# An adaLN block with linear attention on one core: the second modulation vector copied by columns, the first k products of four token tiles run block by block, and the second chunk's transposes put one token tile later

## The chip, the cores and the metric

The kernel runs on one core of a Trainium2 chip. The metric is the device time of one execution in microseconds (us): the median of three runs is 570.62 us (570.37 to 571.47). Beside these runs one execution was recorded by the hardware profiler; it took 570.02 us, and the profile's times are counted from the start of its span.

The engines are TensorE (PE in the rows; PEld are its weight loads), VectorE (DVE), ScalarE (ACT), GpSimd (POOL) and SyncE (SP), which here issues the transfers. Each works through a queue of its own.

## What is computed

The inputs are x (2048 tokens by 512), a condition vector c of 512, and weights. Six modulation vectors of 512 come from `silu(c) @ w_mod`: sa, ca, ga for the attention half, sb, cb, gb for the feed-forward half.

```python
mod = (_silu(c) @ w_mod).reshape(c.shape[0], 6, 1, -1)
h = _layernorm(x, axis=-1) * (1 + ca) + sa
x = x + ga * _A_ref(h, A_wqkv, A_wo)      # linear attention, 32 heads of 16, phi(k), phi(q)
h = _layernorm(x, axis=-1) * (1 + cb) + sb
x = x + gb * _B_ref(h, ...)               # (h W_gate * h W_up) W_down, width 1376
```

In the attention q, k, v are products of h with three 512 x 512 weights. phi(t) is t + 1 for positive t and exp(t) otherwise, plus 1e-6. Over all tokens `kv` sums the products of phi(k) and v, and `z` sums phi(k); a token's output is phi(q) times kv, divided by phi(q) times z, and goes through wo. The change lies in the start of the attention half: ca and sa, the first normalised h, and the first rows of k.

## The kernel before

**Tiling.** The 2048 tokens are four chunks of 512, each of four token tiles of 128 (sixteen tiles, numbered i = 0 to 15). The 512 model columns are four blocks of 128 (b = 0 to 3). A PSUM bank holds 128 x 512 values; there are eight, four in the pool `ps_acc` and four in the pool `ps_w` (`acc_bank()` and `bank()`).

**Split products.** Every float32 operand of a large product is split into a rounded high half and a low half (what is left over): ScalarE copies the high half (`split`, L183), VectorE subtracts to get the low half (L184). One product of a 128-row block is then three TensorE instructions: high by high, high by low, low by high.

**The start.** Chunk 0 is normalised (`Norm`: statistics on VectorE L225 and L226, the power -1/2 on GpSimd L234, the factor `nmr` on VectorE L237, and the scaled tile, called xhat, on ScalarE L243) and turned by TensorE so that the columns lie on the partitions (L257). Meanwhile VectorE multiplies c into the weights of the vectors ca and sa (L159, L161); four small TensorE products (L166, two rows each in the profile) turn the sum into four columns of a PSUM bank, one for each block, and one VectorE instruction (`col_out`, L171) copies them out. Then for each block `modulated` (L259) lets ScalarE write f = scale * xhat + shift (L262), makes its high half h (a VectorE cast, L270, or a second ScalarE instruction, L272) and its low half on VectorE (L273). Fillers (`keep_on`, L143) are products whose result nobody reads, put on TensorE between the small products.

**First products of k.** L365 to L389 write the order out by hand: the copy of sa, the halves of the weight blocks of k (`split_raw(raw_k[b])`) and `modulated` of the four blocks by turns, then `product2` (L200), which runs tiles 0 and 1 together, block after block. Between them stand the statistics of chunk 1 and, for tile 0, the split of xhat (`k_split_x`), `k_phi` (two ScalarE instructions, Relu L291 and Exp L292, then VectorE L295) and the split of phi(k) (`k_split`: kh on ScalarE, L318, kl on VectorE, L319). ScalarE's xhats 0 and 1 of chunk 1 come last.

**The loop over tiles** (L421 to L469). For tile i it issues the product of k for tile i + 2 (`proj`, L196 to L198), for some tiles a product of q, the splits for tile i + 1, the phi of tile i + 2, and `t_tile(i)`: twelve products (L327 to L329) that add xhat by phi(k) into four banks called T. In the first two tiles of a chunk (j = 0 and 1) half of `t_tile` is followed by the transposes of two column blocks of the next chunk (L250) and their `modulated`, then by the other half. At the end of a tile weights are split or modulation vectors summed (`extra`).

**What sets the order.** The schedule is manual: each engine's instructions stand in the order of the source. The waits between engines come from the tiles that they read and write, and a PSUM bank or an SBUF buffer is taken again when its last reader is done. Behind the loop lie the attention's output and the feed-forward half; no line of them is changed.

Of the kernel before, what the change touches and what calls it, by code (L numbers as in the profile page):

```python
# [8 lines left out]
F32 = mybir.dt.float32  # L9
F32R = mybir.dt.float32r  # L10
AF = mybir.ActivationFunctionType
ALU = mybir.AluOpType
AX = mybir.AxisListType

P = 128
# [7 lines left out]
def tile_adaln_block(  # L23
# [12 lines left out]
    nc = tc.nc  # L36
# [3 lines left out]
    KD = D // P  # L40
    NJ = 4
    CH = NJ * P
    NCH = S // CH
# [35 lines left out]
    def acc_bank():  # L79
        return T(ps_acc, "acc")  # L80

    def bank():
        return T(ps_w, "bank")
# [57 lines left out]
    def keep_on(n):  # L141
        for _ in range(n):
            nc.tensor.matmul(ps_idle, idle[:, :P], idle, start=True, stop=True)  # L143
# [19 lines left out]
    def mod_col(acc, ps):  # L163

        for b in range(KD):
            nc.tensor.matmul(ps[:, b:b + 1], acc[:, b * P:(b + 1) * P], ones[:, 0:1], start=True, stop=True)  # L166
        return ps

    def col_out(v, ps, add):
        t = consts.tile([P, KD], F32, name=f"col{v}")  # L170
        nc.vector.tensor_scalar(t, ps[:, :KD], add, None, op0=ALU.add)  # L171
        return t
# [13 lines left out]
    def split_raw(raw, shape=(P, D), low=None):  # L186
        h = B("w", shape, F32R)
        l = B("w", shape, F32R)
        split(raw, h[:raw.shape[0]], l[:raw.shape[0]], low)
        return h, l  # L190
# [6 lines left out]
            nc.tensor.matmul(ps, ah, bl, start=False, stop=False)  # L197
            nc.tensor.matmul(ps, al, bh, start=False, stop=i == n - 1)  # L198

    def product2(pss, pairs):  # L200

        n = len(pairs[0])
        for i in range(n):
            for ps, p in zip(pss, pairs):
                (ah, al), (bh, bl) = p[i]
                nc.tensor.matmul(ps, ah, bh, start=i == 0, stop=False)
                nc.tensor.matmul(ps, ah, bl, start=False, stop=False)
                nc.tensor.matmul(ps, al, bh, start=False, stop=i == n - 1)

    def cut(pair, a, b):  # L210
        return pair[0][:, a:b], pair[1][:, a:b]

# [84 lines left out]
    def k_split_x(i):  # L297
        ch, j = divmod(i, NJ)
        kx[i] = [B("xh", dt=F32R), B("xl", dt=F32R)]
        split(norm[ch].n[j], *kx[i])  # L300

    def k_phi(i, ps):
        phi = B("phi")
        phi_a(ps, phi)
        phi_b(ps, phi)
        phk[i] = phi
# [56 lines left out]
    mod_acc(acc_sa, raw_sa, [0, 1, 2, 3])  # L363
    ca = col_out(1, ps_ca, 1.0)
    keep_on(4)  # L365
    ps_sa = mod_col(acc_sa, acc_bank())
    keep_on(9)
    wk.append(split_raw(raw_k[0]))
    sa = col_out(0, ps_sa, 0.0)
    nx = Norm(xts[1])  # L370
    nx.stats(0)
    n0.modulated(ca, sa, 0, cast=nc.vector)
    wk.append(split_raw(raw_k[1]))
    n0.modulated(ca, sa, 1, cast=nc.vector)
    wk.append(split_raw(raw_k[2]))
    n0.modulated(ca, sa, 2)
    nx.stats(1)
    wk.append(split_raw(raw_k[3]))
    n0.modulated(ca, sa, 3)
    ps0, ps1 = acc_bank(), acc_bank()  # L380
    product2((ps0, ps1), [[(cut(n0.t[k], j * P, (j + 1) * P), wk[k]) for k in range(KD)] for j in range(2)])
    nx.stats(2, 3)
    nx.rstd_of()
    k_split_x(0)
    k_phi(0, ps0)
    nx.nmr_of()
    k_phi(1, ps1)
    k_split(0)
    nx.xhat(0, 1)  # L389

    tacc = [acc_bank() for _ in range(KD)]
    rows, cols = {}, {}
# [24 lines left out]
             13: lambda: (mod_part(5, 0, 1, 2), cols.update({4: col_out(4, mod_col(accs[4], bank()), 1.0)})),  # L417
             14: lambda: (mod_part(5, 3), wo_s.extend(split_raw(x) for x in raw_o)), 15: lambda: rows.update({5: mod_row(5, accs[5])})}
    q_at = {3: 0, 4: 1, 6: 2, 7: 3}
    ahead = {2: proj(2, wk)}  # L420
    for i in range(NT):  # L421
        ch, j = divmod(i, NJ)
        more = ch + 1 < NCH
        if i == 0:
            ahead[3] = proj(3, wk)
        elif i > 1:
            ahead[i + 2] = proj(i + 2, wk) if i + 2 < NT else proj(i + 6 - NT, wq)
        if i in q_at:
            qps = proj(q_at[i], wq)
        if more and j == 0:  # L430
            nx.xhat(2)
        if i + 1 < NT:
            k_split_x(i + 1)
        if more and j == 0:
            nx.xhat(3)
        if i + 1 < NT:
            k_split(i + 1)
        if more and j < 2:
            t_tile(i, 0, 1)
            nx.transpose(2 * j, 2 * j + 1)  # L440
            nx.modulated(ca, sa, 2 * j, 2 * j + 1, cast=nc.vector)
            norm[ch + 1:] = [nx]
        if ch + 2 < NCH and j == 2:
            nx2 = Norm(xts[ch + 2])
            nx2.stats(0, 1)
        if ch + 2 < NCH and j == 3:
            nx = nx2
            nx.stats(2, 3)
            nx.rstd_of()
            nx.nmr_of()  # L450
            nx.xhat(0, 1)
        if i + 2 < NT:
            k_phi(i + 2, ahead.pop(i + 2))
        else:
            q_a(i + 6 - NT, ahead.pop(i + 2))
            q_b(i + 6 - NT)
        if i in q_at:
            q_a(q_at[i], qps)
            q_b(q_at[i])
        if i + 1 < NT:  # L460
            z_add(i + 1)
        if i == NT - 1:
            zps = bank()
            nc.tensor.matmul(zps, ones, zacc, start=True, stop=True)
            zb = consts.tile([P, D], F32, name="zb")
            nc.scalar.activation(zb, zps, AF.Identity, bias=eps_z)
        t_tile(i, *range(2 if more and j < 2 else 0, KD))
        if i in extra:
            extra[i]()  # L469
    ga, gb, sb, cb = rows[2], rows[5], cols[3], cols[4]  # L470
# [727 lines left out]
```

## Time and profile before

| | before |
| --- | --- |
| median of three runs | 570.62 us |
| profiled execution, time | 570.02 us |
| its span | 568.3 us |
| TensorE busy | 560.3 us (99%) |
| VectorE busy | 373.1 us (66%) |
| ScalarE busy | 279.8 us (49%) |
| GpSimd busy | 186.2 us (33%) |

A row of the timeline has the start in us from the span's beginning, the length in us, the engine, the line, the operation with what it writes and reads, and the count; a bracket at its end gives idle time just before it and who ended that. Matmuls are pipelined, so a row's length is longer than the distance to the next one, and their ends are modelled: a wait of TensorE shows best in the distance between starts. Two rows of the same engine may overlap by their start-up.

### The profile page before, as it was taken

How to read it: one execution, taken by the hardware profiler on the slowest of the kernel's cores; microseconds unless marked ns; L12 is line 12 of the kernel's file. 1: busy time of each engine (PE TensorE's matmuls, PEld its weight loads, DVE VectorE, ACT ScalarE, POOL GpSimd, SP SyncE). 2: the span in 40 equal slices, each digit the busy share in tenths (PEclk: the TensorE clock that was granted, in tenths of full speed). 3: DMA queues.
4: the chain of work that ended last, by engine and by line, in shares of the span. 5: the costliest groups of instructions: out<-in, count | busy, mean ns of one | idle time of the engine just before them, and what ended most of it. 6: DMA issues, size and time to landing. Idle time of an engine off the chain costs nothing.

```text
span 568.3 us, 7356 instructions
## 1 busy us (share of the span) xinstructions
PE 560.3 (99%) x2575; PEld 458.8 (81%) x2575; DVE 373.1 (66%) x614; ACT 279.8 (49%) x500; POOL 186.2 (33%) x191
## 2 busy tenths in 40 slices
PE   8999999999999999999989999999999999999997
PEld 6778888888888878878878888787888888888886
DVE  7876868868768876759767777745554434344445
ACT  3785857546456546445865545534333333334110
POOL 2000000000011300000579666665667446556200
PEclk9999999999999999999999999999999999999999
DMA  8900223302301000804208553599336012200004
GB/s 289 374 3 2 74 75 110 114 0 62 93 0 47 29 1 37 260 0 149 57 2 277 180 190 104 202 348 330 115 111 178 26 57 55 57 19 2 0 1 148
DMA packets 50309, 59.34 MB, mean 104 GB/s; under 512 B 6432, under 2 KB 27168, under 8 KB 50272
## 3 DMA queue, kind: packets, MB, share of 16 engines
q1 hardware_dynamic: 50272, 58.87, 32.1%
q8 instruction: 20, 0.33, 0.2%
q14 instruction: 17, 0.14, 0.1%
HBM read 43.12 MB, written 15.73 MB: 104 GB/s over the span
## 4 chain that ended last, share of the span: by engine, by line
PE 89%; DMA 3%; issue 2%; POOL 1%; DVE 1%; ACT 1%; SPq 1%; POOLq 0%; ACTq 0%
PE bank L838 28%; PE acc L914 6%; PE acc L915 6%; PE acc L916 6%; PE acc L614 6%; PE bank L198 5%; PE bank L196 5%; PE bank L197 5%; PE acc L329 3%; PE acc L327 3%; PE acc L328 3%; PE bank L693 2%; PE bank L691 2%; PE bank L692 2%; PE bank L250 2%
## 5 line engine op out<-in xcount | busy, mean ns | idle before, releaser
L838 PE MATMUL bank<-h,w 128*128 128x512 f32 (+1 forms) x798 | 185.5, 390 | 1.8 <-ACT bank L843 1.2
L838 PEld LDWEIGHTS bank<-h,w 128*128 128x128 f32 (+1 forms) x798 | 148.2, 186 | 35.3 <-ACT bank L843 1.7
L843 ACT ACTIVATE bank<-bank 128x512 f32<-128x512 f32 (+1 forms) x38 | 22.1, 583 | 144.8 <-PE bank L838 144.8
L678 DVE TENSOR_TENSOR x<-acc,x 128x512 f32<-128x512 f32 (+1 forms) x73 | 49.1, 684 | 49.0 <-PE acc L916 48.2
L824 POOL TENSOR_TENSOR w<-raw,w 128x256 fp32r<-128x256 f32 (+3 forms) x38 | 42.4, 1117 | 106.4 <-ACT w L817 86.4
L184 POOL TENSOR_TENSOR w<-raw,w 128x512 fp32r<-128x512 f32 (+1 forms) x25 | 34.9, 1399 | 116.0 <-DVE mv L226 87.6
L914 PE MATMUL acc<-w,kh 128*128 128x512 f32 (+2 forms) x154 | 59.6, 387 | 0.0
L915 PE MATMUL acc<-w,kh 128*128 128x512 f32 (+2 forms) x154 | 59.6, 387 | 0.0
L916 PE MATMUL acc<-w,kl 128*128 128x512 f32 (+2 forms) x154 | 59.5, 386 | 0.0
L234 POOL TENSOR_TENSOR rstd<-ve,half 128x4 f32<-128x4 f32 (+1 forms) x9 | 9.4, 1044 | 126.0 <-DVE ve L233 124.5
L184 DVE TENSOR_TENSOR kl<-u,kh 128x512 fp32r<-128x512 f32 (+1 forms) x38 | 26.8, 746 | 33.1 <-ACT kh L183 31.2
L824 POOL TENSOR_TENSOR w<-t,w 128x512 fp32r<-128x512 f32 (+1 forms) x38 | 48.4, 1293 | 0.0
L196 PE MATMUL bank<-w,h 128*128 128x512 f32 x112 | 45.0, 402 | 0.0
L198 PE MATMUL bank<-w,h 128*128 128x512 f32 x112 | 43.9, 392 | 0.0
L197 PE MATMUL bank<-w,h 128*128 128x512 f32 x112 | 43.6, 389 | 0.0
L614 PE MATMUL acc<-w,xh 128*128 128x512 f32 x120 | 38.1, 399 | 0.0
L914 PEld LDWEIGHTS acc<-w,kh 128*128 128x128 f32 (+1 forms) x154 | 28.9, 188 | 6.0
L916 PEld LDWEIGHTS acc<-w,kl 128*128 128x128 f32 (+1 forms) x154 | 28.9, 188 | 5.9
L915 PEld LDWEIGHTS acc<-w,kh 128*128 128x128 f32 (+1 forms) x154 | 28.9, 188 | 5.9
L893 DVE TENSOR_TENSOR u<-bank,u 128x512 f32<-128x512 f32 (+1 forms) x19 | 13.1, 690 | 30.0 <-PE bank L838 30.0
L243 ACT ACTIVATE n<-x,nmr,rstd 128x512 f32<-128x512 f32 x32 | 24.1, 804 | 17.2 <-DVE nmr L237 15.9
L262 ACT ACTIVATE f<-bank,col,col 128x512 f32<-128x512 f32 x28 | 20.7, 775 | 14.5 <-PE bank L250 12.4
(177 smaller groups left out, 1105.1 us busy)
## 6 DMA issues: line engine op xcount, KB each, us to landing
raw<-in_w_mod_dram SPq DMA_DIRECT2D x24, 256.0 KB, 3.7
raw<-in_B_w_down_dram SPq DMA_DIRECT2D x20, 256.0 KB, 2.9
raw<-in_B_w_gate_dram SPq DMA_DIRECT2D x36, 128.0 KB, 3.7
raw<-in_B_w_up_dram SPq DMA_DIRECT2D x36, 128.0 KB, 3.6
x<-in_A_x_dram SPq DMA_DIRECT2D x16, 256.0 KB, 5.4
kept<-f SPq DMA_DIRECT2D x16, 256.0 KB, 2.0
f<-kept SPq DMA_DIRECT2D x16, 256.0 KB, 4.8
side_s<-h SPq DMA_DIRECT2D x16, 256.0 KB, 2.6
```

What stands on the lines that cost most here:

```text
L184: (low or nc.vector).tensor_tensor(l, src, f32(h), op=ALU.subtract)
L196: nc.tensor.matmul(ps, ah, bh, start=i == 0, stop=False)
L197: nc.tensor.matmul(ps, ah, bl, start=False, stop=False)
L198: nc.tensor.matmul(ps, al, bh, start=False, stop=i == n - 1)
L243: nc.scalar.activation(self.n[j], self.tiles[j], AF.Identity, scale=self.rstd[:, j:j + 1], bias=self.nmr[:, j:j + 1])
L614: nc.tensor.matmul(yps[i], x, y, start=False, stop=k == KD - 1 and x is al, skip_group_check=True)
L678: nc.vector.tensor_tensor(xt[:, a:b], dn[j][:, a:b], xt[:, a:b], op=ALU.add)
L824: sub = lambda out, x, y: (on or nc.gpsimd).tensor_tensor(out, x, f32(y), op=ALU.subtract)
L838: mm = lambda x, y, **kw: nc.tensor.matmul(ps, x[:, k], y, skip_group_check=True, **kw)
L914: nc.tensor.matmul(ps, hh[:, a:b], dh[:n, c:d], start=i == 0, stop=False)
L915: nc.tensor.matmul(ps, hh[:, a:b], dl[:n, c:d], start=False, stop=False)
L916: nc.tensor.matmul(ps, hl[:, a:b], dh[:n, c:d], start=False, stop=i == len(hs) - 1)
```

## The change

Three things are edited, all between the sum of sa and the loop's third tile. No transfer and no weight is touched.

1. The four columns of sa are still made by four small products one after the other, but each is copied by an instruction of its own (`sa_out`). The first is copied, block 0 of the weights split and block 0 modulated; then the other three columns are copied. Three fillers follow the small products instead of nine, and all four blocks use VectorE's cast.
2. Tiles 0 to 3 have a bank each from the start (`k_ps`). For blocks 0 and 1 the products of all four tiles run block by block; then blocks 2 and 3 for one tile after the other. `product2` goes, and with it the two `proj` calls for tiles 2 and 3. The statistics of chunk 1, `k_phi` and `k_split` of tiles 0 and 1 are put between in a new order, `k_split(0)` ahead of `k_phi(1)`.
3. The transposes of chunk 1 move from tiles 0 and 1 to tiles 1 and 2. Tile 0 has its twelve T products in one piece; in tile 2 the transposes come first, then all of `t_tile(2)`, then the product of tile 4. The later chunks keep their places.

```diff
-    ps_sa = mod_col(acc_sa, acc_bank())
-    keep_on(9)
-    wk.append(split_raw(raw_k[0]))
-    sa = col_out(0, ps_sa, 0.0)
+    ps_sa = acc_bank()
+    sa = consts.tile([P, KD], F32, name="col0")
+
+    def sa_block(b):
+        nc.tensor.matmul(ps_sa[:, b:b + 1], acc_sa[:, b * P:(b + 1) * P], ones[:, 0:1], start=True, stop=True)
+
+    def sa_out(b):
+        nc.vector.tensor_scalar(sa[:, b:b + 1], ps_sa[:, b:b + 1], 0.0, None, op0=ALU.add)
+
+    def block_in(b):
+        n0.modulated(ca, sa, b, cast=nc.vector)
+
+    def w_in(b):
+        wk.append(split_raw(raw_k[b]))
+
+    for b in range(KD):
+        sa_block(b)
+    keep_on(3)
+    k_ps = [acc_bank(), acc_bank(), bank(), bank()]
+
+    def k_block(b, *js):
+        for j in js:
+            (hh, hl), (wh, wl) = cut(n0.t[b], j * P, (j + 1) * P), wk[b]
+            nc.tensor.matmul(k_ps[j], hh, wh, start=b == 0, stop=False)
+            nc.tensor.matmul(k_ps[j], hh, wl, start=False, stop=False)
+            nc.tensor.matmul(k_ps[j], hl, wh, start=False, stop=b == KD - 1)
+
+    sa_out(0)
+    w_in(0)
+    block_in(0)
+    for b in range(1, KD):
+        sa_out(b)
+    w_in(1)
+    block_in(1)
+    k_block(0, 0, 1, 2, 3)
     nx = Norm(xts[1])
+    w_in(2)
+    block_in(2)
     nx.stats(0)
-    n0.modulated(ca, sa, 0, cast=nc.vector)
-    wk.append(split_raw(raw_k[1]))
-    n0.modulated(ca, sa, 1, cast=nc.vector)
-    wk.append(split_raw(raw_k[2]))
-    n0.modulated(ca, sa, 2)
+    k_block(1, 0, 1, 2, 3)
+    w_in(3)
+    block_in(3)
     nx.stats(1)
-    wk.append(split_raw(raw_k[3]))
-    n0.modulated(ca, sa, 3)
-    ps0, ps1 = acc_bank(), acc_bank()
-    product2((ps0, ps1), [[(cut(n0.t[k], j * P, (j + 1) * P), wk[k]) for k in range(KD)] for j in range(2)])
-    nx.stats(2, 3)
+    k_split_x(0)
+    k_block(2, 0)
+    k_block(3, 0)
+    nx.stats(2)
+    k_phi(0, k_ps[0])
+    k_block(2, 1)
+    k_block(3, 1)
+    nx.stats(3)
     nx.rstd_of()
-    k_split_x(0)
-    k_phi(0, ps0)
+    k_split(0)
+    k_phi(1, k_ps[1])
     nx.nmr_of()
-    k_phi(1, ps1)
-    k_split(0)
     nx.xhat(0, 1)
+    k_block(2, 2)
+    k_block(3, 2)
+    k_block(2, 3)
+    k_block(3, 3)
...
-    ahead = {2: proj(2, wk)}
+    ahead = {2: k_ps[2], 3: k_ps[3]}
+    turn_at = {4 * ch + j: (ch + 1, 2 * j, 2 * j + 1) for ch in range(1, NCH - 1) for j in range(2)}
+    turn_at.update({1: (1, 0, 1), 2: (1, 2, 3)})
     for i in range(NT):
...
-        if i == 0:
-            ahead[3] = proj(3, wk)
-        elif i > 1:
+        done = 0
+        if i > 2:
             ahead[i + 2] = proj(i + 2, wk) if i + 2 < NT else proj(i + 6 - NT, wq)
...
-        if more and j < 2:
-            t_tile(i, 0, 1)
-            nx.transpose(2 * j, 2 * j + 1)
-            nx.modulated(ca, sa, 2 * j, 2 * j + 1, cast=nc.vector)
-            norm[ch + 1:] = [nx]
+        if i in turn_at:
+            to, *ks = turn_at[i]
+            if i != 2:
+                t_tile(i, 0, 1)
+                done = 2
+            nx.transpose(*ks)
+            nx.modulated(ca, sa, *ks, cast=nc.vector)
+            norm[to:] = [nx]
+        if i == 2:
+            t_tile(i, *range(KD))
+            done = KD
+            ahead[i + 2] = proj(i + 2, wk)
...
-        t_tile(i, *range(2 if more and j < 2 else 0, KD))
+        t_tile(i, *range(done, KD))
```

More of the change, by code (lines that the diff above doesn't have):

```diff
@@ L198, in product @@
             nc.tensor.matmul(ps, al, bh, start=False, stop=i == n - 1)
[L200 to L208, printed above, removed]
     def cut(pair, a, b):
@@ L419, in tile_adaln_block @@
     q_at = {3: 0, 4: 1, 6: 2, 7: 3}
-    ahead = {2: proj(2, wk)}
+    ahead = {2: k_ps[2], 3: k_ps[3]}
+    turn_at = {4 * ch + j: (ch + 1, 2 * j, 2 * j + 1) for ch in range(1, NCH - 1) for j in range(2)}
+    turn_at.update({1: (1, 0, 1), 2: (1, 2, 3)})
     for i in range(NT):
         ch, j = divmod(i, NJ)
-        more = ch + 1 < NCH
-        if i == 0:
-            ahead[3] = proj(3, wk)
-        elif i > 1:
+        done = 0
+        if i > 2:
             ahead[i + 2] = proj(i + 2, wk) if i + 2 < NT else proj(i + 6 - NT, wq)
@@ L429, in tile_adaln_block @@
             qps = proj(q_at[i], wq)
-        if more and j == 0:
+        if ch + 1 < NCH and j == 0:
             nx.xhat(2)
@@ L433, in tile_adaln_block @@
             k_split_x(i + 1)
-        if more and j == 0:
+        if ch + 1 < NCH and j == 0:
             nx.xhat(3)
```

## The prediction

> **What bounds the kernel now.** I read the page first (share of the span by engine), then TensorE's rows in order of time, then those of VectorE and ScalarE in the same stretch, and last what the chain of waits says of the rest. The page:
>
> ```profile
> PE 560.3 (99%) x2575; PEld 458.8 (81%) x2575; DVE 373.1 (66%) x614; ACT 279.8 (49%) x500; POOL 186.2 (33%) x191
> ```
>
> TensorE is the bound, but a share over the span says nothing of the first 45 us, where the change lies. The timeline of TensorE there (start, length, line):
>
> ```profile
> 14.94 1.05 PE L166 MATMUL acc<-ones,f 128*128 128x1 f32 x8
> 15.85 2.34 PE L143 MATMUL acc<-w 128*128 128x512 f32 x9
> 18.03 0.39 PE L206 MATMUL acc<-w,h 128*128 128x512 f32 x1
> 18.26 0.40 PE L207 MATMUL acc<-w,h 128*128 128x512 f32 x1
> ...
> 20.01 0.50 PE L208 MATMUL acc<-w,h 128*128 128x512 f32 x1
> ...
> 29.71 0.39 PE L327 MATMUL acc<-kh,xh 128*128 128x512 f32 x1
> ...
> 31.08 1.04 PE L250 MATMUL bank<-ident,n 128*128 128x128 f32 x8
> 31.87 0.47 PE L327 MATMUL acc<-kh,xh 128*128 128x512 f32 x1
> ...
> 43.03 0.39 PE L196 MATMUL bank<-w,h 128*128 128x512 f32 x1
> ```
>
> The nine fillers end, the first product starts at 18.03, and by 43.03 TensorE has done 96 products (48 of k for tiles 0 to 3, 36 of T for tiles 0 to 2, 12 of k for tile 4) and 16 transposes. A product starts 0.23 after the one before it (18.03 to 18.26; I count 0.2285, the mean where they run on, so 96 come to 21.94), eight transposes take 0.87 (the L250 start, less the 0.16 overlap of its row's 1.04), so the work is 23.68 of 25.00 us: 1.32 of waits. What fed it is VectorE's queue:
>
> ```profile
> 8.46 0.17 DVE L233 TENSOR_SCALAR ve<-mv 128x2 f32<-128x2 f32 x1
> 8.54 0.16 DVE L151 TENSOR_SCALAR ce<-ce 128x4 f32<-128x4 f32 x1
> ...
> 14.87 0.68 DVE L184 TENSOR_TENSOR w<-raw,w 128x512 fp32r<-128x512 f32 x1
> 16.03 0.16 DVE L171 TENSOR_SCALAR col<-acc 128x4 f32<-128x4 f32 x1 [0.47 <-PE acc L166]
> ...
> 17.17 0.40 DVE L270 CAST h<-f 128x512 fp32r<-128x512 f32 x1
> 17.60 0.69 DVE L273 TENSOR_TENSOR h<-f,h 128x512 fp32r<-128x512 f32 x1
> 18.21 0.69 DVE L184 TENSOR_TENSOR w<-raw,w 128x512 fp32r<-128x512 f32 x1
> ...
> 19.26 0.69 DVE L273 TENSOR_TENSOR h<-f,h 128x512 fp32r<-128x512 f32 x1
> ...
> 21.08 0.69 DVE L225 BATCH_NORM_STATS2 st<-x 128x6 f32<-128x512 f32 x1
> ...
> 21.90 0.67 DVE L184 TENSOR_TENSOR w<-raw,w 128x512 fp32r<-128x512 f32 x1
> ...
> 24.83 0.17 DVE L233 TENSOR_SCALAR ve<-mv 128x4 f32<-128x4 f32 x1
> ...
> 26.49 0.16 DVE L237 SCALAR_TENSOR_TENSOR nmr<-mv,rstd 128x4 f32<-128x4 f32 x1 [0.30 <-POOL rstd L234]
> ...
> 29.62 0.69 DVE L184 TENSOR_TENSOR xl<-n,xh 128x512 fp32r<-128x512 f32 x1 [1.77 <-ACT xh L183]
> ```
>
> VectorE is all but full from 17.17 to 27.85, and only then idles for long (1.77, before 29.62). The spacings are my prices: a 512-wide subtract, add or phi step 0.60 (17.60 to 18.21), a cast 0.45, statistics with their aggregate 0.82 (21.08 to 21.90), a small one 0.08 (8.46 to 8.54); ve to nmr, by way of GpSimd's power, 1.66. ScalarE's queue:
>
> ```profile
> 16.23 0.78 ACT L262 ACTIVATE f<-bank,col,col 128x512 f32<-128x512 f32 x1 [1.96 <-DVE col L171]
> 16.90 0.62 ACT L183 ACTIVATE w<-raw 128x512 fp32r<-128x512 f32 x1
> 17.42 0.77 ACT L262 ACTIVATE f<-bank,col,col 128x512 f32<-128x512 f32 x1
> ...
> 19.27 0.78 ACT L272 ACTIVATE h<-bank,col,col 128x512 fp32r<-128x512 f32 x1
> ...
> 23.76 0.60 ACT L291 ACTIVATE phi<-acc 128x512 f32<-128x512 f32 x1 [1.33 <-PE acc L208]
> 24.39 0.64 ACT L292 ACTIVATE phi<-phi 128x512 f32<-128x512 f32 x1
> 24.93 0.58 ACT L291 ACTIVATE phi<-acc 128x512 f32<-128x512 f32 x1
> ...
> 26.23 0.72 ACT L318 ACTIVATE kh<-phi,eps_phi 128x512 fp32r<-128x512 f32 x1
> 26.85 2.21 ACT L243 ACTIVATE n<-x,nmr,rstd 128x512 f32<-128x512 f32 x3
> 28.97 0.62 ACT L183 ACTIVATE xh<-n 128x512 fp32r<-128x512 f32 x1
> 29.49 0.80 ACT L243 ACTIVATE n<-x,nmr,rstd 128x512 f32<-128x512 f32 x1
> 30.20 0.71 ACT L318 ACTIVATE kh<-phi,eps_phi 128x512 fp32r<-128x512 f32 x1
> ```
>
> Prices here: f 0.67, copy 0.52, Relu 0.63, Exp 0.54, kh 0.63, xhat 0.71 (26.85 to 28.97 is three). See that all four xhats of chunk 1 stand ahead of tile 1's kh (30.20), and that nmr is what starts them. Handing on costs 0.03 between ScalarE and VectorE, 0.20 after a small column write (16.03 to 16.23), and 0.16 into a product that waits (the low half of 19.26 is done at 19.95, the product's row starts at 20.01 and is 0.11 longer than the 0.39 of others).
>
> **The change, part by part.** Nothing moves on a DMA queue; on SP's queue nothing is added or passed. GpSimd only gets its one power later.
>
> (1) The copy by columns. ps_sa's four products come all before the first copy, in one PSUM bank. If the first copy waits for all four, it runs at 16.03 as now. If it waits for its own column alone, it runs after two of the eight L166 rows: (1.05 − 0.19)/7 = 0.123 a row, so 0.74 earlier. I take the first: the nearest row, L171, starts 0.04 after the last of the eight, and no row shows one engine reading a bank that another is writing. The Trainium skill, "PSUM — Partial Sum Buffer", section "PSUM bank collisions raise a hardware error", says that bank accesses of two engines are to be guarded by bank (and quadrant), not by address, disjoint columns included. By that rule the gain here is 0; no run here shows it.
>
> Three copies more cost 3 x 0.08 = 0.24. Before, the low half of weight block 0 ran at 14.87, under the wait for L171; now it stands behind the first copy: 0.60 of cover lost, half of it (0.32) again under the wait for f.
>
> (2) Blocks 2 and 3 take a VectorE cast in place of ScalarE's L272: VectorE +0.90, ScalarE −1.33 (it waits anyway). The six fillers fewer (1.37) only become idle time: the first product waits for the cast.
>
> (3) The queues walked forward, each start the later of the engine's last and of what it needs. VectorE: copy 16.03; low of w0 16.11; cast 0 17.04 (f's 16.23 + 0.78 + 0.03); low of h0 17.48; copies 18.08 to 18.24; low of w1 18.32. ScalarE's f1 now waits for the second copy: 18.28 (17.42 before), so cast 1 19.09, low 19.54; w2 20.14; cast 2 20.74, low 21.19; statistics 0 21.79; w3 22.61; cast 3 23.21, low 23.66; statistics 1 24.26; xl of tile 0 25.08; statistics 2 25.68; phi of tile 0 26.50; statistics 3 27.10; ve 27.9 to 28.06; kl of tile 0 next.
> TensorE: cast 0 done 17.46, first product 17.62, the third waits for the low half (18.17 + 0.16 = 18.33: 0.26 wait), and the other 45 follow at 0.2285 without one (the tightest operand, the low half of h3, is usable at 23.66 + 0.69 + 0.16 = 24.51, and its turn comes at 18.33 + 27 x 0.2285 = 24.50): T of tile 0 starts at 28.84 (before: 29.71), a lead of 0.87, and as all four of its blocks now stand together it ends at 31.58.
>
> (4) Tile 1 is not there. Exp of tile 1 is behind kh of tile 0 on ScalarE, and that waits for phi of tile 0: kh 27.21, Relu 27.84, Exp 28.47, done 29.10; phi of tile 1 on VectorE 29.13; nmr is behind it, 29.73 (ve + 1.66 gives the same 29.7). Before: 26.49. ScalarE: xhat 29.92, three of them 2.12, xh 32.04, xhat 32.56, kh of tile 1 33.27, done 33.99; TensorE 34.15. It waits 34.15 − 31.58 = 2.57, and 0.26 more for kl. Before, the 24 products of tiles 2 and 3 ran while ScalarE came to this kh, and eight transposes stood amid T of tile 0; now those products are spent earlier and the transposes come after, so nothing covers it.
>
> (5) The rest of the stage: ten products, 16 transposes and T of tile 2 end at 41.64; six products of tile 4, 43.01. Its block 2 is late: Relu 2 33.90, Exp 34.53, phi 2 on VectorE 35.19, then from phi 2 on ten steps of 0.60 (phi, sum, a half of q's weights, xl and kl, for tile 2 and again for tile 3) and two casts with their lows (2.10) between: cast 43.29, product 43.87: waits 0.86, 0.26, 0.10, 0.26. End 45.87.
>
> The sum against before's stage: first product 17.62 for 18.03, −0.41; waits 0.26 + 2.57 + 0.26 + 0.86 + 0.26 + 0.10 + 0.26 = 4.57 for 1.32, +3.25; together +2.84 (45.87 for 43.03). The same walk over before's order ends at 42.75, 0.28 early, so 2.84 to 3.12; I take +3.0. Carried on to tile 8 the walk shows both orders at this distance and no new wait.
>
> Behind it the kernel keeps the distance if nothing there has a clock of its own. The one stretch where TensorE waits long, near 290, hangs on a load that SP issues when TensorE lets go (chain of waits, then TensorE's row):
>
> ```profile
> 264.18 0.25 PE acc L717
> 264.42 0.02 SPq L110
> ```
>
> ```profile
> 292.19 3.02 PE L838 MATMUL bank<-h,w 128*128 128x512 f32 x12 [1.24 <-ACT bank L843]
> ```
>
> so it moves along. The profiled execution took 570.02 (span 568.3), 0.60 under the median; 573.0 by its own count, 573.6 against the median 570.62.
>
> **The rivals.**
> A, copied by columns in earnest: the first copy at 15.29. VectorE and TensorE start 0.74 earlier, and so does all of (3) to (5): +2.3, 572.9. For it: each copy names one column. Against it: the bank is shared.
>
> B, the clock falls in the 2.57 us pause. The cold start bounds it:
>
> ```profile
> 1.99 7.58 PE L143 MATMUL acc<-w 128*128 128x512 f32 x20 [1.99 <-DVE w L138]
> ```
>
> 20 fillers took 7.58 where warm ones take 4.57: up to 3.0 lost, so 573.6 to 576.6, about 575.5. Against it: the twelve products after the 1.24 pause at 292.19 took 3.02, 0.24 each, full speed. The longest pause inside before is half of this one. The Trainium skill, "TensorE: Matmul & The Clock Gate", Part 1, has the clock halve after an idle window of about 3.4 us; by that 2.57 is too short and B would be 0. No row here has a pause so long.
>
> C, faster: kh of tile 1 doesn't wait behind the xhats, because ScalarE gets to it before nmr is there (an order by readiness and not as written). Then T of tile 1 and, since the same queue then runs ahead, tile 4 find their operands, and TensorE has no wait after 18.33: 18.33 + 94 x 0.2285 + 1.74 = 41.55, 1.48 ahead: 569.1. It decides where nmr is there by 27.1, or kh needs none. Against it: before's rows stand as written in the source, kh of tile 1 (30.20) behind the last xhat too.
>
> D, part is given back later: TensorE's waits near 290 (1.24 here) shrink as it comes later. Up to 1.3 of 3.0: 572.3. Against it: the load is set off by TensorE itself (264.18 to 264.42).
>
> **How the numbers follow.** Forecast 0.63, A 0.14, B 0.08, C 0.06, D 0.09 (a third of it down to no change). The measurement tells about 0.2% (1.1 us) from no change. Faster 0.06, same 0.04, slower 0.90. The range 571.8 to 575.1 takes in the forecast with some 0.7 of error in the walk, A, and D as priced, and leaves out C, full give-back and most of B.
>
> **What would show it.** The first column copy after the last L166 row (right) or after the second (A). TensorE's first product near 17.6, T of tile 0 near 28.8, then a wait of 2 to 3 us on kh of tile 1, with ScalarE's xhats just before it and nmr near 29.7; a wait of about 0.9 on VectorE's cast in tile 4. After that the rows of after lie 3 us behind those of before up to the end. Wrong if nmr comes by 27, if no wait stands before tile 1, or if the clock is under 1.00 behind the pause.

## The result and the profile after

The changed kernel takes 573.28 us (median of 6, 572.07 to 574.19) where before takes 570.50 beside it (median of 6, 569.61 to 571.47): a ratio of 1.0047, 95% interval 1.0032 to 1.0062. It is slower by 0.47%, and the interval leaves no change out. Its profiled execution took 572.73 us with a span of 571.0, 2.7 more than the span of before. The page's totals after:

```profile
PE 558.7 (98%) x2569; PEld 456.7 (80%) x2569; DVE 373.7 (65%) x619; ACT 278.6 (49%) x498; POOL 185.7 (33%) x191
```

TensorE does no more work (558.7 us for 560.3; it has six fillers fewer), so the span is longer by waiting alone. TensorE's timeline of the changed kernel (start, length, engine, line, operation; in brackets the idle time ahead and its releaser) shows where:

```profile
14.74 1.05 PE L360 MATMUL acc<-ones,f 128*128 128x1 f32 x8
...
17.32 0.50 PE L379 MATMUL acc<-w,h 128*128 128x512 f32 x1 [0.73 <-DVE h L260]
...
18.04 0.50 PE L381 MATMUL acc<-w,h 128*128 128x512 f32 x1
...
28.76 0.39 PE L317 MATMUL acc<-kh,xh 128*128 128x512 f32 x1
...
31.25 0.39 PE L319 MATMUL acc<-kl,xh 128*128 128x512 f32 x1
33.91 0.50 PE L317 MATMUL acc<-kh,xh 128*128 128x512 f32 x1 [2.27 <-ACT kh L308]
...
43.66 0.50 PE L196 MATMUL bank<-w,h 128*128 128x512 f32 x1 [0.60 <-DVE h L260]
...
45.78 0.40 PE L196 MATMUL bank<-w,h 128*128 128x512 f32 x1
```

The stage from the start of ps_sa's products to tile 5's first product (the 97th product, as 43.03 is in before) took 45.78 − 14.74 = 31.04 us; before's took 43.03 − 14.94 = 28.09. The start of ps_sa's products lies anywhere between 14.31 and 15.24 in the profiles of this case, which is why the stage is counted from it. The first product comes 0.71 earlier and T of tile 0 0.95 earlier (28.76 for 29.71). All of that, and more, is lost between 31.25 and 33.91, where T of tile 1 waits for its kh. The profile's bracket counts idle time from the modelled end of the product before; from start to start it is 33.91 − 31.25 − 0.23 = 2.43 us. A second wait, at 43.66, is for VectorE's cast in tile 4.

VectorE's queue after, and ScalarE's, say why kh of tile 1 was late:

```profile
15.83 0.16 DVE L363 TENSOR_SCALAR col<-acc 128x1 f32<-128x1 f32 x1 [1.07 <-PE acc L360]
...
27.91 0.17 DVE L223 TENSOR_SCALAR ve<-mv 128x4 f32<-128x4 f32 x1
...
29.00 0.69 DVE L285 SCALAR_TENSOR_TENSOR phi<-acc,phi 128x512 f32<-128x512 f32 x1 [0.33 <-ACT phi L282]
29.61 0.15 DVE L227 SCALAR_TENSOR_TENSOR nmr<-mv,rstd 128x4 f32<-128x4 f32 x1
```

```profile
29.80 2.23 ACT L233 ACTIVATE n<-x,nmr,rstd 128x512 f32<-128x512 f32 x3 [0.83 <-DVE nmr L227]
31.93 0.61 ACT L183 ACTIVATE xh<-n 128x512 fp32r<-128x512 f32 x1
32.45 0.80 ACT L233 ACTIVATE n<-x,nmr,rstd 128x512 f32<-128x512 f32 x1
33.16 0.71 ACT L308 ACTIVATE kh<-phi,eps_phi 128x512 fp32r<-128x512 f32 x1
```

nmr comes at 29.61 (26.49 in before), because VectorE reaches ve only at 27.91 (24.83) and phi of tile 1 only at 29.00. The four xhats wait for nmr, and kh of tile 1 stands behind the fourth.

### The profile page after: what moved, and what is told of

Same layout as the page of the kernel before. It is cut to its first block, busy times and chain, and to the rows that moved or that the text cites. A ratio compares the mean times of both kernels' runs of the same rounds, so it can differ in the third digit from the quotient of the medians.

```text
span 571.0 us, 7354 instructions
## 1 busy us (share of the span) xinstructions
PE 558.7 (98%) x2569; PEld 456.7 (80%) x2569; DVE 373.7 (65%) x619; ACT 278.6 (49%) x498; POOL 185.7 (33%) x191
## 4 chain that ended last, share of the span: by engine, by line
PE 85%; ACT 4%; DVE 3%; issue 3%; DMA 2%; POOL 1%; SPq 1%; POOLq 0%; DVEq 0%
PE bank L871 27%; PE acc L948 6%; PE acc L947 6%; PE acc L949 6%; PE acc L647 6%; PE bank L196 5%; PE bank L198 5%; PE bank L197 5%; PE acc L319 2%; PE acc L317 2%; PE acc L318 2%; PE bank L726 2%; PE bank L724 2%; PE bank L725 2%; PE bank L240 2%
## 5 line engine op out<-in xcount | busy, mean ns | idle before, releaser
L196 PE MATMUL bank<-w,h 128*128 128x512 f32 x104 | 42.0, 403 | 0.6 <-DVE h L260 0.6
L198 PE MATMUL bank<-w,h 128*128 128x512 f32 x104 | 40.8, 392 | 0.0
L197 PE MATMUL bank<-w,h 128*128 128x512 f32 x104 | 40.5, 389 | 0.0
L317 PE MATMUL acc<-kh,xh 128*128 128x512 f32 x64 | 26.0, 406 | 2.3 <-ACT kh L308 2.3
```

Of the source, the lines that this page charges most:

```text
L317: nc.tensor.matmul(tacc[k], xh[:, a:b], kh, start=first, stop=False)
```

## The experiments

In the experiments the hand-written order, from ps_sa to the end of tile 2, stands as a list of calls, one to a line, and the loop starts at tile 3. sa_out(b) copies one column and sa_all() all four; w_in(b) and q_in(b) split a block of k's and of q's weights; block_in(b) makes f, cast and low half of block b with the cast on VectorE, block_act(b) with the cast on ScalarE; k_block(b, tiles) is block b's products for these tiles; xh_of, xl_of, kh_of and kl_of make the halves of a tile; exp_of(i) runs Relu and Exp of a tile and t_tile its T products; k_turned(b) modulates a transposed block. The diffs are against the changed kernel in this form, but for e1 and e11. The stage in the table is that of the profiled execution, from the start of ps_sa's products to tile 5's first product. The last column counts the executions whose mean granted clock was 0.997 or less.

| kernel | median us | ratio to before (95%) | stage us | clock ≤ 0.997 |
|---|---|---|---|---|
| before | 570.5 to 570.7 | 1 | 28.09 | 1 of 61 |
| after | 573.28 | 1.0047 (1.0032–1.0062) | 31.04 | 4 of 6 |
| e1_copies | 570.37 | 0.9999 (0.9990–1.0009) | 28.97 | 0 of 10 |
| e2_one_copy | 572.40 | 1.0032 (1.0020–1.0043) | 31.18 | 4 of 6 |
| e3_tiles23_late | 572.43 | 1.0033 (1.0020–1.0046) | 31.03 | 3 of 5 |
| e4_kh_first | 573.68 | 1.0066 (1.0040–1.0092) | 30.44 | 2 of 4 |
| e5_turns_early | 572.52 | 1.0032 (1.0021–1.0043) | 30.24 | 4 of 7 |
| e6_own_bank | 571.78 | 1.0021 (1.0012–1.0031) | 30.30 | 8 of 10 |
| e7_three_moves | 571.03 | 1.0010 (0.9999–1.0020) | 29.23 | 2 of 10 |
| e8_order | 568.54 | 0.9966 (0.9953–0.9979) | 28.21 | 4 of 10 |
| e9_filled | 572.94 | 1.0042 (1.0028–1.0056) | 31.03 | 1 of 6 |
| e10_order_filled | 568.00 | 0.9958 (0.9946–0.9970) | 26.75 | 0 of 5 |
| e11_before_again | 570.75 | 1.0000 (0.9991–1.0009) | 28.09 | 1 of 10 |
| e12_order_own | 567.77 | 0.9951 (0.9938–0.9963) | 25.93 | 0 of 5 |

The profiled executions of e2 and e8 are among those with a lower clock, and their stages hold it.

**Does the listed form change anything?** e11_before_again is before's order in this form, with no edit.

> The kernel before's instructions in their order, written with the helpers of the experiments: ratio 1.000, first product of tile 5 at 43.0. It shows how far two profiles and two sets of runs of one program lie apart; what lies behind the stage should take 525.3 us as in the first profile if that was typical, and about 0.6 us more if the first profile was a fast one.

570.75 for 570.67, and the same 28.09 us of stage, so the form costs nothing. But behind the stage this execution took 525.9 us (span 568.9, tile 5 at 42.97), where the first profile of before took 525.3: by the expectation's own test that first profile was a fast one, by some 0.6 us. Where the 0.6 us lie is shown with rival D below.

**Which part costs?** e1_copies is before with the copy by columns (and one tile's statistics moved behind the copies), e2_one_copy the changed kernel without it and without the casts and fillers that came with it.

```diff
 # e1_copies, against before
+sa_out(0)
 w_in(0)
-sa_all()
-nx.stats(0)
 block_in(0)
+sa_out(1)
+sa_out(2)
+sa_out(3)
+nx.stats(0)
```

> The kernel before with only the copy by columns put in (first column, low half of the first weight block, block 0, then three more copies; the nine fillers, the block order of the products and the transposes as before). By the walk along the queues VectorE comes to block 1 about 1 us later, TensorE waits 1.0 us for it inside the first products of tiles 0 and 1, and the stage to the first product of tile 5 ends 1.1 us later than before (44.1 for 43.0): about +1.0 us in the time, no part of it from a bank conflict. If the copies cost only their own length (three times 0.08 us), the time is within 0.3 us of before. If the first copy really ran 0.74 us earlier, the stage would end no later than before.

```diff
 # e2_one_copy
-keep_on(3)
+keep_on(9)
-sa_out(0)
 w_in(0)
+sa_all()
 block_in(0)
-sa_out(1)
-sa_out(2)
-sa_out(3)
 ...
-block_in(2)
+block_act(2)
 ...
-block_in(3)
+block_act(3)
```

> The changed kernel with the first part undone: one copy of all four columns after nine fillers, the low half of the first weight block ahead of it, and ScalarE's second instruction for the high half of blocks 2 and 3, as before; order of the products, statistics and transposes as changed. If the loss comes from the copies, the time is back near before (about 2 us under the changed kernel). By the walk it is not: nmr is still behind phi of tile 1, TensorE still waits about 2.35 us for kh of tile 1, and the stage ends only 0.2 us earlier than in the changed kernel (45.6): about +2.6 us over before.

The copies alone lengthen the stage by 0.88 us, by waits for casts that come later (TensorE's timeline of e1):

```profile
20.08 0.50 PE L402 MATMUL acc<-w,h 128*128 128x512 f32 x1 [0.64 <-DVE h L260]
```

but the median doesn't show it (−0.1 ± 0.5 us, where 1.0 was expected); 0.6 of it is given back later, below. Taking the copies out of the changed kernel lowers the median by 0.9 us of the 2.8, but the two intervals overlap, and at full clock the two kernels don't differ (two executions each: 572.13 and 572.59 for 572.07 and 572.73). So most of the loss is in the rest of the change. VectorE's queue in e2 shows where it is late:

```profile
25.87 0.69 DVE L285 SCALAR_TENSOR_TENSOR phi<-acc,phi 128x512 f32<-128x512 f32 x1 [1.05 <-ACT phi L282]
...
27.41 0.17 DVE L223 TENSOR_SCALAR ve<-mv 128x4 f32<-128x4 f32 x1
...
29.11 0.15 DVE L227 SCALAR_TENSOR_TENSOR nmr<-mv,rstd 128x4 f32<-128x4 f32 x1
```

From the start of ps_sa's products nmr comes after 14.63 us here (29.11 − 14.48), after 14.87 in the changed kernel, after 11.55 in before. With the copies and casts undone VectorE has 1.05 us to spare and spends it waiting for Exp of tile 0, because phi of tile 0 now stands ahead of the last statistics and of ve; in before all statistics and ve come first (24.83) and phi after. No run moves the statistics alone back.

**Do the copies wait for the bank or for their column (rival A)?** The first column gets a PSUM bank of its own.

```diff
 # e6_own_bank
-ps_sa = acc_bank()
+ps_sa, ps_s0 = acc_bank(), acc_bank()
 ...
-  matmul(ps_sa[:, b:b + 1], ...)
+  matmul((ps_sa if b else ps_s0)[:, b:b + 1], ...)
 ...
-  tensor_scalar(sa[:, b:b + 1], ps_sa[:, b:b + 1], ...)
+  tensor_scalar(sa[:, b:b + 1], (ps_sa if b else ps_s0)[:, b:b + 1], ...)
```

> The changed kernel with the first column's product in a PSUM bank of its own, so that its copy waits for that product alone. If copies wait by bank, the first copy moves from 0.04 us after the last of the eight rows to about 0.04 us after the second (0.74 us earlier), everything behind it moves by as much, and the time falls by 0.7 us against the changed kernel (stage end 45.0). If they already waited by column, nothing changes.

In the changed kernel the first copy stands at 15.83, behind the last of the eight rows of ps_sa (14.74 + 1.05 = 15.79). TensorE's timeline of e6:

```profile
14.71 1.05 PE L360 MATMUL acc<-ones,f 128*128 128x1 f32 x8
...
16.71 0.47 PE L402 MATMUL acc<-w,h 128*128 128x512 f32 x1
```

The first copy stands at 15.13, 0.42 after the start of these rows (1.09 in the changed kernel). From ps_sa to the first product are 2.00 us in place of 2.58, and the stage is 0.74 shorter, the price in the prediction's step (1): six rows of 0.123. The median is 1.5 lower, more than that explains; at full clock the two kernels are 1.0 apart (571.23 and 571.64 for 572.07 and 572.73). So the copy of one column waited for every product into its bank. acc_bank() hands out one tile of the program with each bank, and e6 gives the column both: whether the wait hangs on the bank or on the tile is open.

**Is the wait for kh a lack of cover?** By the prediction's step (4), the products of tiles 2 and 3 are spent early and leave nothing to cover ScalarE. e3 puts blocks 0 and 1 of those tiles back behind all products of tiles 0 and 1.

```diff
 # e3_tiles23_late
-k_block(0, 0, 1, 2, 3)
+k_block(0, 0, 1)
 ...
-k_block(1, 0, 1, 2, 3)
+k_block(1, 0, 1)
 ...
 nx.xhat(1)
+k_block(0, 2)
+k_block(1, 2)
 k_block(2, 2)
 k_block(3, 2)
+k_block(0, 3)
+k_block(1, 3)
```

> The changed kernel with the products of tiles 2 and 3 in one piece behind those of tiles 0 and 1, as before; VectorE and ScalarE in the changed order. If the wait for kh of tile 1 comes from the lost cover (24 products that used to run while ScalarE got to it), it goes and the time falls by about 2.4 us. By the walk it shrinks to 0.2 us, but waits of 0.4, 0.3, 0.3, 1.5 and 0.3 us for VectorE's blocks come in its place inside the products of tiles 0 and 1, since the same queue is late: the stage ends where it does in the changed kernel (45.8), and the time is the same, about +2.8 us over before.

The wait at tile 1 is gone, and the stage is as long as before the edit, to 0.01 us. The median is 0.85 lower, where none was expected, but the intervals overlap and at full clock the times are the changed kernel's (572.16 and 572.70 for 572.07 and 572.73). The loads of weights in e3 show where it went:

```profile
19.44 0.19 PEld L402 LDWEIGHTS acc<-w,h 128*128 128x128 f32 x1 [0.64 <-DVE h L260]
...
23.58 0.19 PEld L402 LDWEIGHTS acc<-w,h 128*128 128x128 f32 x1 [1.56 <-DVE h L260]
...
43.65 0.19 PEld L196 LDWEIGHTS bank<-w,h 128*128 128x128 f32 x1 [1.02 <-DVE h L260]
```

The same idle time now stands between the blocks, for VectorE's casts. So the lost cover isn't the cause; VectorE and ScalarE are late, and TensorE waits for them at one place or at another.

**What of the two queues is late?** e4 makes kh of tile 1 ahead of the xhats; e5 puts the first transposes back amid T of tile 0; e7 makes three moves in the two queues.

```diff
 # e4_kh_first
 nx.nmr_of()
+xh_of(1)
+xl_of(1)
+kh_of(1)
+kl_of(1)
 nx.xhat(0)
 ...
 nx.xhat(2)
-xh_of(1)
-xl_of(1)
 nx.xhat(3)
-kh_of(1)
-kl_of(1)
 # e5_turns_early
+t_tile(0, 0, 1)
+nx.transpose(0)
+nx.transpose(1)
+k_turned(0)
+k_turned(1)
 ...
-t_tile(0, 0, 1, 2, 3)
+t_tile(0, 2, 3)
 ...
 t_tile(1, 0, 1)
-nx.transpose(0)
-nx.transpose(1)
-k_turned(0)
-k_turned(1)
+nx.transpose(2)
+nx.transpose(3)
+k_turned(2)
+k_turned(3)
 ...
-nx.transpose(2)
-nx.transpose(3)
-k_turned(2)
-k_turned(3)
 # e7_three_moves
 nx.nmr_of()
+xh_of(1)
 ...
 nx.xhat(2)
-xh_of(1)
 xl_of(1)
-nx.xhat(3)
 kh_of(1)
 kl_of(1)
 exp_of(2, k_ps[2])
+nx.xhat(3)
 ...
-kl_of(3)
 ...
 k_turned(3)
+kl_of(3)
```

> The changed kernel with both splits of tile 1 (xh, xl, kh, kl) put ahead of the four xhats of chunk 1 on ScalarE and VectorE. If the place of kh behind the xhats is the whole of the loss, the 2.3 us wait goes and the time falls by 2.3 us or more. By the walk the wait goes, but the transposes then wait for the xhats (0.3 and 1.2 us) and tile 4 waits 1.7 us for its block 2 in place of 0.9: the stage ends 0.6 us earlier (45.1), about +2.1 us over before.

> The changed kernel with the transposes of chunk 1 back in tiles 0 and 1 (the third part undone). By the walk they now wait for the xhats one after the other (0.7, 0.6, 0.6 and 1.1 us at the four token tiles), since nmr is still near 29.6; tile 4 waits only 0.6 us. The stage ends 0.8 us earlier than in the changed kernel (45.0): about +2.0 us over before. If the later transposes were the cause, the time would be back at before.

> The changed kernel with three moves: xh and xl of tile 1 right behind nmr, the last xhat of chunk 1 behind Relu and Exp of tile 2 (so behind kh of tile 1), and kl of tile 3 behind the blocks 2 and 3 of tile 4. By the walk the wait for kh of tile 1 falls to 1.4 us and that for tile 4 to 0.4 us; the stage ends 1.8 us earlier (44.0), about +1.0 us over before. If the queues' order is not the cause, the time stays.

Loads of weights in e4:

```profile
37.13 0.42 PEld L240 LDWEIGHTS bank<-ident,n 128*128 128x128 f32 x4 [1.11 <-ACT f L252]
43.41 0.19 PEld L196 LDWEIGHTS bank<-w,h 128*128 128x128 f32 x1 [1.93 <-DVE h L260]
```

in e5:

```profile
30.75 0.14 PEld L240 LDWEIGHTS bank<-ident,n 128*128 128x128 f32 x1 [0.79 <-ACT n L233]
31.46 0.14 PEld L240 LDWEIGHTS bank<-ident,n 128*128 128x128 f32 x1 [0.57 <-ACT n L233]
32.16 0.14 PEld L240 LDWEIGHTS bank<-ident,n 128*128 128x128 f32 x1 [0.57 <-ACT n L233]
33.38 0.53 PEld L240 LDWEIGHTS bank<-ident,n 128*128 128x128 f32 x5 [1.09 <-ACT n L233]
```

and in e7:

```profile
33.17 0.19 PEld L317 LDWEIGHTS acc<-kh,xh 128*128 128x128 f32 x1 [1.46 <-ACT kh L380]
...
42.34 0.19 PEld L196 LDWEIGHTS bank<-w,h 128*128 128x128 f32 x1 [0.44 <-DVE h L260]
```

In e4 the wait at tile 1 is gone and the transposes and tile 4's cast, now later, wait in its place: the stage is 0.60 shorter, the median no lower than after's (572.87 and 572.64 at full clock, 574.50 and 575.63 in the two executions with a lower one). In e5 the transposes wait for one xhat after the other; the stage is 0.80 shorter and the median 0.8. e7 shortens both of after's waits, 2.70 to 1.46 and 1.03 to 0.44 in the loads of weights, for 1.81 us of stage and 2.3 of the median (with a lower clock in 2 of 10 executions for 4 of 6). No single move removes the wait: each shifts most of it to the next late operand, and what is left over is the gain.

**Can four tiles per block be fast?** e8 keeps the changed kernel's k products and puts the two queues into an order (the diff has some of its moves) found by walking them forward as the prediction did: one copy, blocks 2 and 3 cast by ScalarE, kh of tile 1 ahead of the xhats, halves of tile 1 and 2 between the statistics, all of T of tile 1 ahead of the first transposes. e10 is e8 with six fillers for three. e12 adds the first column's own bank, with four fillers, one copy for each column and its order walked anew (its other moves are not in the diff).

```diff
 # e8_order
-block_in(2)
+block_act(2)
 ...
 nx.nmr_of()
+q_in(1)
+kh_of(1)
 nx.xhat(0)
 ...
 t_tile(1, 0, 1)
+t_tile(1, 2, 3)
 nx.transpose(0)
 ...
 # e10_order_filled, against e8
-keep_on(3)
+keep_on(6)
 # e12_order_own, against e10
-keep_on(6)
+keep_on(4)
-ps_sa = acc_bank()
+ps_sa, ps_s0 = acc_bank(), acc_bank()
 ...
```

> The changed kernel's four products per block with a new order of VectorE's and ScalarE's work up to tile 3: one copy, the low half of the first weight block ahead of it, ScalarE's own high half for blocks 2 and 3, the copies of tile 1 and tile 2 and two of q's weight blocks in ScalarE's idle time before the first Relu, kh of tile 1 ahead of the xhats, lower halves where VectorE idles. By the walk TensorE waits only for the first cast and its low half, the stage ends 4.2 us earlier than in the changed kernel (41.5), and the time is about 1.5 us under before. If the queue order is not what bounds the stage, it is not faster than before.

> The new order of e8_order with six fillers in place of three ahead of the first product. Of e8_order's executions those with a mean clock of 0.996 or 0.997 took 569.6 to 570.0 and the others 567.8 to 568.9. If the short pause ahead of the first product lets the clock fall, the slower group is gone and the median is 568.0 to 568.2. If it has another cause, both groups stay and the median is near 568.5.

> The new order joined with the first column's product in a bank of its own, copied alone, and four fillers, so that no pause is left. By the walk TensorE's first product is at 16.6 to 16.7, it waits 0.3 us for the first low half and 0.2 us at T of tile 0, and the stage ends 0.7 us earlier than in e8_order without a fall of the clock: 567.3, some 3.2 us under before. If the first copy were not what the stage waits for, it is no faster than e10_order_filled.

e8 is 0.34% faster than before, and its ten executions fall into two groups: 567.79 to 568.91 at a mean clock of 0.999 or more (six), 569.57 to 569.98 at 0.996 or 0.997 (four). Its profiled execution is of the second group. Its load of weights ahead of the first product, TensorE's timeline, and the view of stretches (busy time of TensorE, of its weight loads, of VectorE, ScalarE and GpSimd, then granted clock, share of DMA, GB/s):

```profile
17.37 0.19 PEld L405 LDWEIGHTS acc<-w,h 128*128 128x128 f32 x1 [1.15 <-DVE h L260]
```

```profile
17.37 0.50 PE L405 MATMUL acc<-w,h 128*128 128x512 f32 x1 [0.72 <-DVE h L260]
...
18.10 0.79 PE L407 MATMUL acc<-w,h 128*128 128x512 f32 x1
18.69 0.63 PE L405 MATMUL acc<-w,h 128*128 128x512 f32 x1
19.12 0.63 PE L406 MATMUL acc<-w,h 128*128 128x512 f32 x1
```

```profile
15.00:17.30 2.30, 1.65 (x11) 1.17 (x10) 0.98 (x3) 1.22 (x3) 0.00 (x0) 1.00 1.05 387
17.30:18.30 1.00, 0.93 (x3) 0.50 (x4) 0.96 (x3) 1.00 (x3) 0.00 (x0) 0.77 1.06 389
18.30:21.30 3.00, 3.00 (x8) 2.32 (x9) 2.97 (x6) 3.00 (x6) 0.00 (x0) 0.51 1.05 386
21.30:30.00 8.70, 8.70 (x40) 7.19 (x39) 6.56 (x15) 5.47 (x10) 0.67 (x1) 1.00 0.84 308
```

The clock is at half from about 18 to 21.3, and products start 0.43 apart in place of 0.23, for 1.4 to 1.5 us in all: e10, at full clock, has a stage 1.46 shorter (26.75 for 28.21). The pause ahead of the first product had been 0.72 us long by TensorE's row, 1.15 in its loads of weights. In e10 three more fillers leave 0.48 of it, all five executions are at 0.999 or more, and the group at 569.6 and above is gone: 568.00. Five are few: if 4 in 10 still fell, none of five would come about once in 13. e12, at 567.77, has the lowest median, 2.9 us under before (0.49%; 3.2 expected), though its executions overlap e10's. TensorE's timeline in e12 has next to no waits in the stage:

```profile
17.04 0.47 PE L402 MATMUL acc<-w,h 128*128 128x512 f32 x1
...
40.97 0.39 PE L196 MATMUL bank<-w,h 128*128 128x512 f32 x1
```

**Is after's loss the clock's?** e9 is the changed kernel with six fillers for three ahead of the first product and ten between T of tile 0 and of tile 1; the pause of 1.0 us in tile 4 stays unfilled.

```diff
 # e9_filled
-keep_on(3)
+keep_on(6)
 ...
 t_tile(0, 0, 1, 2, 3)
+fill = bank()
+for _ in range(10):
+    nc.tensor.matmul(fill, idle[:, :P], idle, start=True, stop=True)
```

> The changed kernel with both pauses of TensorE filled by products that nobody reads: six fillers in place of three ahead of the first product, and ten between T of tile 0 and T of tile 1, into a bank of their own. No real product moves, so the stage ends where it does in the changed kernel. If executions of the changed kernel lose about 1 us more when the clock falls to half behind a pause (mean clock 0.993 to 0.997 in its record), none does so here: mean clock 0.998 or more in all, and a median some 0.9 us under the changed kernel's, 572.4. If the clock falls for another reason, the spread and the median stay (573.3).

The median, 572.94, is half a microsecond above the 572.4 that I had expected of it, its interval overlaps after's, and the stage is as long as after's. Five of six executions are at full clock (571.91 to 573.10); the sixth, at 0.996, took 574.55. The mean of the five is 572.6, for 570.67: about 2 us of the loss are there without any loss of clock.

## Why the prediction was right, and where its sizes were off

The forecast was 573.6, slower; it is 573.28. The mechanism held up to tile 5. That the number came so close is in part luck, as the last paragraph of this section says.

Step (1), the copy waits for the whole bank: shown, by the row at 15.83 and by e6 (bank or tile, as said there). Rival A is out. The Trainium skill, "PSUM — Partial Sum Buffer", section "PSUM bank collisions raise a hardware error", has such accesses guarded by bank and quadrant; e6 fits it, with 0.74 us, but doesn't tell the bank from the tile.

Steps (2) and (3), the walk of the queues: less the earlier start of ps_sa (0.20), each of these rows came within 0.2 us. First product 17.32 for 17.62, the third 18.04 for 18.33, T of tile 0 28.76 for 28.84, nmr 29.61 for 29.73, tile 5's first product 45.78 for 45.87.

Step (4), the wait at tile 1: 2.43 for 2.57, released by kh of L308 as said; the order of the rows on ScalarE speaks against C. But the last sentence of that step, that cover was missing since the products were spent early, was the wrong reason: with the cover put back (e3) the loss is the same. Both queues are about 3 us late (nmr 14.87 us after ps_sa's products for 11.55), and each order of TensorE's work that was tried with these queues (after, e3, e5) pays 2.2 to 3.0 us for that.

Step (5), tile 4: 43.66 for 43.87, and the stage is 2.95 longer (2.75 as the clock times stand) where I had 2.84 to 3.12.

Rival B, the clock: under-rated at 0.08, though the median isn't explained by it alone. The profiled execution of after has full clock throughout, as I had expected, but four of six executions are at 0.993 to 0.996, and take 573.00 to 574.19 where the two others take 572.07 and 572.73: about 1 us. None of the four was profiled, so which pause it was is open. I had asked only whether the 2.57 us pause would do it, and priced it at up to 3.0. The fall in e8's profile follows a pause of 1.15 us ahead of the first product, that in e2's one of 2.50 at tile 1 (e2's loads of weights, then its view of stretches, columns as above):

```profile
33.41 0.19 PEld L317 LDWEIGHTS acc<-kh,xh 128*128 128x128 f32 x1 [2.50 <-ACT kh L380]
```

```profile
31.00:34.00 3.00, 0.93 (x4) 0.30 (x2) 1.30 (x2) 2.97 (x6) 0.00 (x0) 1.00 0.00 0
34.00:37.00 3.00, 3.00 (x10) 2.39 (x10) 2.55 (x6) 2.16 (x4) 0.00 (x0) 0.53 0.00 0
```

By the idle window of about 3.4 us in the Trainium skill, "TensorE: Matmul & The Clock Gate", Part 1, both pauses are too short; these rows disagree with it as I had read it. That page also has the window run freely. That could be why only some executions fall, if a window that is idle in part can count, which Part 1 doesn't say; no run here shows the window itself. Step (2) had said that six fillers fewer become idle time and nothing else. e8 and e10 show that this is not all: with three fillers 4 of 10 executions take some 1.7 us longer than the rest, with six none of 5; and of the changed kernel itself, filled in e9, 1 of 6 falls for 4 of 6, too few to be sure.

Rival D, part is given back later: right in kind, wrong in place. The wait near 290 stayed (1.2 us), but between the two first profiles the changed kernel gains 0.57 near 365 and loses 0.6 near 310. In before TensorE pauses for VectorE's u near 366. Its rows on TensorE, VectorE and GpSimd:

```profile
366.77 1.65 PE L838 MATMUL bank<-h,w 128*128 128x512 f32 x6 [0.28 <-DVE u L893]
```

```profile
364.90 1.22 DVE L184 TENSOR_TENSOR h<-f,h 128x512 fp32r<-128x512 f32 x1 [0.64 <-ACT w L817]
```

```profile
364.83 0.74 POOL L824 TENSOR_TENSOR w<-raw,w 128x256 fp32r<-128x256 f32 x1 [5.52 <-ACT w L817]
```

and in the changed kernel, on the same three engines:

```profile
361.41 9.73 PE L871 MATMUL bank<-h,w 128*128 128x512 f32 x42
```

```profile
367.81 0.69 DVE L184 TENSOR_TENSOR h<-f,h 128x512 fp32r<-128x512 f32 x1 [0.29 <-ACT h L183]
```

```profile
368.09 1.02 POOL L857 TENSOR_TENSOR w<-raw,w 128x256 fp32r<-128x256 f32 x1 [5.51 <-ACT w L850]
```

In before GpSimd starts 0.07 ahead of VectorE, and VectorE's subtract takes 1.22 us; in after VectorE starts 0.28 ahead, takes 0.69, and GpSimd takes 1.02 in place of 0.74. TensorE then runs 42 products without a break. The other way round near 310, where VectorE starts second after waiting 0.91 for a load (0.38 in before), and TensorE waits (after's timeline):

```profile
309.54 1.65 PE L871 MATMUL bank<-h,w 128*128 128x512 f32 x6 [0.35 <-DVE u L926]
```

So the span is 2.75 + 0.6 − 0.57 later, 2.7 within the rounding. But the loss near 310 isn't the change's. e11 runs before's instructions in their order, and its profile has the same break (TensorE, then VectorE's row ahead of it; last, VectorE's row at that place in the first profile of before):

```profile
306.84 1.65 PE L951 MATMUL bank<-h,w 128*128 128x512 f32 x6 [0.34 <-DVE u L1006]
```

```profile
304.98 1.21 DVE L869 TENSOR_TENSOR s<-f,f 128x512 f32<-128x512 f32 x1 [0.64 <-DMA f<-kept]
```

```profile
304.80 0.77 DVE L756 TENSOR_TENSOR s<-f,f 128x512 f32<-128x512 f32 x1 [0.38 <-DMA f<-kept]
```

GpSimd's product starts at 304.90 in e11 and at 304.98 in before: in the one VectorE comes second and takes 1.21, in the other first and takes 0.77. One order does both, so this 0.6 us comes and goes with the execution; why the load comes earlier or later is open. Of the 14 profiles 8 have the break near 310 (after, e1, e3, e5, e8, e9, e11, e12). The break near 365 is different: both executions of before's order have it (366.77, and 367.34 in e11), none of the 12 others does. So the 0.57 is given back in every changed order. It takes most of e1's 0.88 us away (e1's and e11's spans are both 568.9), which is why the median doesn't show them. No run set the two engines against each other on purpose.

Two things that the likeliest case had left out went in opposite directions. The clock goes with about 1 us more in four of six executions, and some 0.6 us is given back near 365. Against e11's profile, which has the break near 310 as after's has, the stage is 2.95 longer (2.81 as the clock times stand) but the span only 2.1 (571.0 for 568.9); at full clock the times are 1.9 apart (the mean of 572.07 and 572.73, for 570.5). So the step "behind it the kernel keeps the distance" didn't hold, and +3.0 for the whole was about 1 us too much for a full clock. The first profile of before, without the break, hid that: against it the span is 2.7 longer. The walk was right for the stage; that the median came within 0.3 us is luck as well, since the lower clock put back what the later stretch gave away.

## What to carry to other kernels

Price a reordering by walking the in-order queues of the engines that feed the bound, each start the later of the engine's last and of its operands; the cover of the bounding engine's own work tells only where the wait will show, not whether. When one wait is removed, look for the same time at the next operand before calling it a gain. Where fillers cost nothing, cover a pause of TensorE of even about a microsecond: e8 lost 1.5 us behind one. Give a value that is needed early a PSUM bank (and tile) of its own. And profile one order twice before a difference of half a microsecond far behind the edit is put down to the edit.

## What the runs showed of the hardware

The granted clock can fall to half for some 3 us after pauses of 1.15 and 2.50 us, in some executions of a kernel and not in others (4 of 10 of e8, none of 5 when the pause was filled; 1 of 61 of before, 1 of 10 of e11). Not every such pause does it: e1 has one of 1.06 us in its loads of weights (0.64 in TensorE's row at 20.08), and none of its ten executions fell; which pauses do is open. Nor does a lower mean clock always cost time. In e2 the four executions at 0.996 or 0.997 took 571.88 to 572.53 and the two others 572.13 and 572.59, in e3 three took 572.34 to 572.46 and two 572.16 and 572.70. In e7 the means lie 1.5 apart, in e8 1.7; in e6 0.5 (eight executions with a lower clock, two without).

A two-operand VectorE instruction that starts 0.07 us behind a GpSimd one took 1.22 us in place of 0.69, and a GpSimd one that starts 0.28 behind VectorE's took 1.02 in place of 0.74. In the first case GpSimd's row ends at 365.57 and VectorE's 0.55 later, in the second VectorE's at 368.50 and GpSimd's 0.61 later: by these ends the second works only when the first is done. The Trainium skill, "SBUF — State Buffer", section "SBUF: two separate sides", has such a pair of engines share ports under an exclusive lock; these rows agree with it.
